# Last chunk's up product over 256 full rows: seven half-width block products in place of eight

## The chip, the core and the metric

The kernel runs on one core of a Trainium2 chip. The metric is the device time of one execution in microseconds (us). Five engines with queues of their own work side by side: TensorE (PE in the profile; its weight loads are listed apart as PEld), VectorE (DVE), ScalarE (ACT), GpSimd (POOL) and SyncE (SP, which here only issues DMAs). Each engine takes its instructions in the order of the program and waits for others through semaphores.

## What is computed

A recurrent attention cell over 4 batches, 8 heads and 768 time steps of 40 dimensions gives `y`; its heads are laid side by side as 3072 tokens of 320 values, and these go through a gated feed-forward block:

```python
x = attn_out.transpose(0, 2, 1, 3).reshape(B * S, H * D)   # 3072 x 320
h = x @ w_in                                               # 320 x 2048
g = h * np.cos(h)
return g @ w_out                                           # 2048 x 320
```

The change concerns `x @ w_in`, called the up product here. `g @ w_out` is the down product.

## The kernel before

The 768 time steps are cut into six chunks of 128. One chunk of all four batches is 512 tokens. While chunk `c` goes through the feed-forward block, the cells of chunk `c + 1` are computed beside it; the last chunk, `c = 5`, has no cell work beside it.

`both_parts(c, b)` runs two of a chunk's eight steps, `f2 = 2b` and `2b + 1`. A step makes 256 of the 2048 columns of `h`, in two PSUM banks of 128 columns by 512 tokens (`pup`, `self.pu[0]` and `[1]`, from a pool of two buffers, so that the next step needs these two banks again). In each step:

- `Up` issues the up product. The 320 rows of `w_in` are two blocks of 128 rows (`w_in_sb`, line 659) and 64 rows that are left over (`w_in_l`, line 653). A block takes the full 512 tokens against 128 columns: four products of 128x512 per step, then two products of 64 rows. Each float32 product is two passes on TensorE, so that the profile counts 8 and 4.
- `near` (ScalarE, line 667) rounds `h`, `rest` (VectorE, line 670) takes the remainder, `sin` (ScalarE, line 675) its sine, and `gate` (VectorE, line 679) multiplies by `h`. This is done for both banks; the last reading of a bank is by `gate`.
- `sums` adds halves of the gated tiles, on VectorE (lines 728 to 731) and beside it on GpSimd (lines 733 to 736). They feed the down product, which is already made of seven block products in place of eight. GpSimd's first sum waits for the second `gate`.
- `down_slot` issues a number of the down product's parts, each of 160 columns (line 769), for earlier steps: the last chunk has 14 for each of its 8 steps. `quota` says how many in which step; the sums of the last step are used after the loop.

At `f2 = 0` of a chunk the 12 products that are left of the chunk before are issued; then `combine_first` and `combine` (lines 781 to 799) add up its four accumulators `X0, X1, Y0, Y1` into the output tiles. They lie in a PSUM pool of four banks. At `f2 = 1` sixteen `late` products of the chunk before follow, in a bank that comes free when `combine` has read `X0` (line 789).

The order of each engine's queue is the order in which the program is written (`tc.manual_schedule()`). In a step of the last chunk it is: up product on TensorE, the four element-wise steps, `sums`, `down_slot`. `x` of a chunk lies in `xT` (blocks of 128 rows, index `NK * b + i`) and `xL` (the 64 rows); line 548 writes the last part of `xT` for the next chunk during step 6 of the chunk before.

Three pools matter here beside these: `raws` (`qr`, `kr`, the raw q and k of two cells at a time), which are last read when the last cells are transposed (line 457); `pe` with tag `E`, three buffers of 128x1024; and GpSimd's queue in chunk 4, which also carries `scale_q` (line 466) and `decay_exponents` (line 391), the latter followed by eight exponentials on ScalarE (line 405).

Of the kernel before, what the change touches and what calls it, by code (L numbers as in the profile page):

```python
# [11 lines left out]
FP = mybir.dt.float32  # L12
# [17 lines left out]
def kernel(  # L30
# [610 lines left out]
    class Up:  # L641


        def __init__(self, c, f2):
            self.c, self.f2 = c, f2
            self.pu = [ps_u.tile([128, B * C], FP, name="pup", tag="up") for _ in range(2)]

            ahead = f2 % 2 == 1 and c < NC - 1

            def low():  # L650
                for e, pu in enumerate(self.pu):
                    r = slice(64 * e, 64 * e + 64)
                    nc.tensor.matmul(pu, w_in_l[r, f2], xL[c][r].rearrange("p b t -> p (b t)"), start=ahead, stop=not ahead)  # L653

            if ahead:
                low()
            for i in range(NK):
                for e, pu in enumerate(self.pu):
                    nc.tensor.matmul(pu.rearrange("p (b t) -> p b t", b=B), w_in_sb[:, i, ts(2 * f2 + e, 128)], xT[c][:, i:NK * B:NK],  # L659
                                     start=(i == 0 and not ahead), stop=(i == NK - 1 and ahead))  # L660
            if not ahead:
                low()
            self.n = [p3.tile([128, B * C], I32, name="n", tag="n") for _ in range(2)]
# [13 lines left out]
        def gate(self, e):  # L677
# [2 lines left out]
                                           op0=OP.mult, op1=OP.mult)  # L680
            gs[self.c, 2 * self.f2 + e] = g

    def down(c, f2):
        if f2 == 0:
            po[c] = [ps_o.tile([128, DM], FP, name="po", tag="o") for _ in range(B)]

        order = [(f, b) for f in (2 * f2, 2 * f2 + 1) for b in range(B)]
        if f2 == NF // 2 - 1:
            order.sort(key=lambda fb: fb[1])
        for f, b in order:  # L690
            nc.tensor.matmul(po[c][b], gs[c, f][:, ts(b, C)], w_out_sb[:, f], start=(f == 0), stop=(f == NF - 1))  # L691
            if f == NF - 1:
                o = out_tile()
                nc.scalar.copy(out=o, in_=po[c][b])
                out_to(c, b, o)
# [11 lines left out]
    def weight_sums(part):  # L707

        if part == 0:
            for i in range(3):  # L710
                T[i] = pc.tile([128, NF // 2, HALF], FP, name=f"T{i}", tag="bits")
        r = ts(part, NF // 8)
        B11, B12, B21, B22 = (wv[:, r, e, h] for e in range(2) for h in range(2))
        T2, T3, T4 = (t[:, r] for t in T)
        nc.gpsimd.tensor_tensor(out=T3, in0=B22, in1=B12, op=OP.subtract)
        nc.gpsimd.tensor_tensor(out=B12, in0=B12, in1=B11, op=OP.subtract)
        nc.gpsimd.tensor_tensor(out=T2, in0=B22, in1=B12, op=OP.subtract)
        nc.gpsimd.tensor_tensor(out=T4, in0=B21, in1=T2, op=OP.subtract)
# [41 lines left out]
    def late_products(c):  # L760
        L = late[c] = ps_o.tile([128, 2, HALF], FP, name="late", tag="o")
        for k in range(NF // 2):
            for i, rhs in ((0, wv[:, k, 0, 1]), (1, wv[:, k, 1, 1])):
                yield L[:, i], Ds[c, k // 4][:, k % 4, i], rhs, k == 0 and i == 0, k == LAST and i == 1

    def run(made, n):
        for _ in range(n):
            a, lhs, rhs, start, stop = next(made)
            nc.tensor.matmul(a, lhs, rhs, start=start, stop=stop)  # L769
# [39 lines left out]

    made_of = {}  # L810

    def down_slot(c, f2):

        if c == 0:
            if f2 > 0:
                down(0, f2 - 1)
            return
        if f2 == 0:
            if c == 1:
                down(0, LAST)  # L820
            else:
                run(made_of[c - 1], 12)
            return
        if f2 == 1 and c > 1:
            run(late_products(c - 1), NF)
            combine_late(c - 1)
            return
        if c not in made_of:
            made_of[c] = all_products(c)
        each = 14 if c == NC - 1 else 12  # L830
        quota = [0] * 8
        for m in range(2, 8):
            quota[m] = each * 7 * (m - 1) // 6 - each * 7 * (m - 2) // 6
        run(made_of[c], each if c == 1 else quota[f2])

    pw, pmu = (ps_u.tile([128, HP, C], FP, name=name, tag="up") for name in ("pw", "pmu"))
# [199 lines left out]
    def both_parts(c, b):  # L1036

        n = (c + 1) * B + b
        cell = n < N
        for i in range(2):  # L1040
            f2 = 2 * b + i
            up = Up(c, f2)
            if cell and i == 0:
                scores(n)
            if cell and i == 1:
                if n % 2 == 1 and n > B + 1 and n + 3 < N:
                    load_two(n + 3, "Kv")
            for e in range(2):
                up.near(e)
            for e in range(2):  # L1050
                up.rest(e)
            if i == 0:
                if cell:
                    weigh(n)
                    if n + 1 < N:
                        decay_exponents(n + 1)
                for e in range(2):
                    up.sin(e)
                    up.gate(e)
                if c > 0:  # L1060
                    sums(c, f2)
                if b == 0 and c == 1:
                    sigmoid(c + 1)

                if c == 0:
                    made = [pieces.pop(0) for _ in range(min(1, len(pieces)))]
                    p, piece = outs.pop(0)
                    made.append(piece)
                    for dst, bits in made:
                        take_apart(dst, bits)  # L1070
                    for dst, bits in made:
                        bound(dst)
                    for dst, bits in made:
                        put_together(dst, bits)
                    load_out(p)
                if cell and n + 1 < N:
                    decay(n + 1)
            else:
                if cell:
                    seam_out(n)  # L1080
                if cell:
                    state(n)
                for e in range(2):
                    up.sin(e)
                    up.gate(e)
                if c > 0:
                    sums(c, f2)
                if n == B + 1:
                    low_dimensions(n + 1)
                if pieces:  # L1090
                    to_float32(*pieces.pop(0))
                if cell and n + 1 < N:
                    if c > 0:
                        weigh_k(n + 1)
                    odd_values(n + 1)
            if i == 1 and b == B - 1 and 0 < c < NC - 2:
                sigmoid(c + 2)
                sin_next()
            down_slot(c, f2)
            if f2 == 0 and c > 1:  # L1100
                for p in range(2):
                    combine_first(c - 1, p)
            if cell and i == 0:
                turn_gate(n)
                values(n)
                seam(n)
                normalize_turned(n)
                fade(n)
                if c == 1 and b < 3:
                    weight_sums(b + 1)  # L1110
                if n % 2 == 1 and n > B + 1 and n + 3 < N:
                    load_two(n + 3, "qk")
                if n > B + 1 and n + 3 < N:
                    load_E(n + 3)
                if b == B - 2 and c + 2 < NC:
                    load_o(c + 2)
                if c == 0 and pieces:
                    to_float32(*pieces.pop(0))
                sin_next()
            if f2 == 0 and c > 1:  # L1120
                for p in range(2):
                    combine(c - 1, p)
            if i == 1:
                if c == 0 and b + 2 < B:
                    pieces.extend(weights_in(b + 2))
                    load_two((n + 3) // 2 * 2)
                    load_E(n + 3)
                if c == 0:
                    turn_blocks(n + 1, "k")
                    p = next_out()  # L1130
                    turn_blocks(n + 1, "q")
                    scale_q(n + 1)
                    weigh_k(n + 1)
                    load_out(p)
                elif cell and n + 1 < N:
                    turn_blocks(n + 1)
                    scale_q(n + 1)
                if (c, f2) == (0, LAST):
                    weight_sums(0)

    pieces, outs = [], []
    with tc.manual_schedule():
# [41 lines left out]
```

## Time and profile before

| | us |
|---|---|
| three runs | 533.92, 536.92, 536.73 (median 536.73) |
| span of the profiled execution (no other time of it is listed) | 535.1 |
| TensorE busy over the span | 519.7 (97%) |
| VectorE, ScalarE, GpSimd busy | 419.1, 287.1, 226.5 |
| chunk 5, from its first up product to the last down product | 453.84 to 529.9 |
| its eight up products, 128-row part | 3.5 each |
| its eight up products, 64-row part | 1.06 each |

A group of the profile is read as: line, engine, operation, tile written and tiles read, shapes, count, busy time and mean of one. In a timeline, the first number is the start in us, the second how long the group took; matmuls overlap their neighbours by their pipeline, so that the distance between two starts is the time that they occupy.

### The profile page before, as it was taken

Reading aid. Unit: us, or ns where it says so; the run is one execution under the profiler, and the core shown is the slowest. Engines: PE = TensorE matmul, PEld = TensorE weight load, DVE = VectorE, ACT = ScalarE, POOL = GpSimd, SP = SyncE. Lnnn points to the kernel's source line nnn. Section 1 sums busy time; section 2 is a strip of 40 time slices with the busy share of each in tenths; the row PEclk is TensorE's granted clock in tenths of the full one; section 3 lists DMA queues with packets and bytes.
Section 4 is the critical chain, followed back from the end, with each engine's and each line's share of the span. In section 5 each row is a group of like instructions: output and inputs, shape, how many; then the busy total and the mean of one; then the engine's idle time right before and its main releaser. Section 6 shows DMA issues by size and latency. Waiting matters only on the chain.

```text
span 535.1 us, 10497 instructions
## 1 busy us (share of the span) xinstructions
PE 519.7 (97%) x3844; PEld 353.6 (66%) x3844; DVE 419.1 (78%) x907; ACT 287.1 (54%) x548; POOL 226.5 (42%) x369
## 2 busy tenths in 40 slices
PE   7999889999999999999999999999999999999996
PEld 4886446556657767667667667667667667576755
DVE  5565988997888888898878898878897878663636
ACT  2586987857556537835537736527835531322221
POOL 7435554654676572632632632632431422121211
PEclk9586989999999999999999999999999999999999
DMA  9998859769949359139159239159210000000001
GB/s 138 233 205 221 256 143 219 172 108 248 174 115 196 40 131 190 45 93 184 40 119 164 54 89 187 38 118 164 56 59 7 2 5 6 26 26 1 0 1 49
DMA packets 99939, 57.81 MB, mean 108 GB/s; under 512 B 62304, under 2 KB 92608, under 8 KB 99888
## 3 DMA queue, kind: packets, MB, share of 16 engines
q1 hardware_dynamic: 96496, 55.64, 48.3%
q10 hardware_dynamic: 3248, 1.33, 1.2%
q8 instruction: 30, 0.49, 0.4%
q14 instruction: 21, 0.17, 0.1%
q0 software_dynamic: 144, 0.18, 0.1%
HBM read 51.71 MB, written 4.11 MB: 104 GB/s over the span
## 4 chain that ended last, share of the span: by engine, by line
PE 85%; DVE 6%; ACT 4%; issue 2%; DMA 2%; POOL 1%; SPq 1%; DVEq 0%; POOLq 0%; ACTq 0%
PE pup L659 28%; PE acc L769 24%; PE pup L653 8%; PE po L691 5%; PE ps L484 4%; PE late L769 3%; PE vt L519 2%; PE ph L500 2%; PE vt L510 2%; PE pu L611 2%; PE pt L434 1%; PE pw L841 1%; DMA bits<-in_moe_w_in_dram 1%; PE pm L376 1%; PE vt L516 1%
## 5 line engine op out<-in xcount | busy, mean ns | idle before, releaser
L659 PE MATMUL pup<-xT,w_in_sb 128*128 128x512 f32 x384 | 176.0, 601 | 0.2
L667 ACT ACTIVATE n<-pup 128x512 int32<-128x512 f32 x96 | 53.8, 593 | 187.1 <-PE pup L653 135.6
L659 PEld LDWEIGHTS pup<-xT,w_in_sb 128*128 128x128 f32 x384 | 70.1, 191 | 86.4 <-issue 84.2
L670 DVE SCALAR_TENSOR_TENSOR n<-pup,n 128x512 f32<-128x512 f32 x96 | 63.1, 687 | 73.0 <-ACT n L667 71.6
L733 POOL TENSOR_TENSOR D<-g 128x128 f32<-128x128 f32 x40 | 19.8, 496 | 217.3 <-DVE g L679 217.3
L675 ACT ACTIVATE n<-n 128x512 f32<-128x512 f32 x96 | 57.6, 627 | 23.1 <-DVE n L670 14.6
L679 DVE SCALAR_TENSOR_TENSOR g<-pup,n 128x512 f32<-128x512 f32 x96 | 61.7, 684 | 3.9 <-ACT n L675 3.3
L769 PE MATMUL acc<-w_out_sb,g 128*128 128x160 f32 x320 | 58.6, 304 | 0.0
L769 PE MATMUL acc<-T,g 128*128 128x160 f32 x320 | 58.0, 301 | 0.1
L653 PE MATMUL pup<-xL,w_in_l 64*128 64x512 f32 x192 | 54.2, 641 | 0.0
L769 PEld LDWEIGHTS acc<-w_out_sb,g 128*128 128x128 f32 x320 | 47.7, 190 | 5.6 <-issue 4.2
L769 PEld LDWEIGHTS acc<-T,g 128*128 128x128 f32 x320 | 48.1, 190 | 3.7 <-issue 3.0
L405 ACT ACTIVATE E<-E,tab 128x128 f32<-128x128 f32 x160 | 49.0, 388 | 0.3
L691 PE MATMUL po<-w_out_sb,g 128*128 128x320 f32 x128 | 37.7, 449 | 4.1 <-POOL w_out_sb L165 4.1
L691 PEld LDWEIGHTS po<-w_out_sb,g 128*128 128x128 f32 x128 | 24.7, 196 | 16.3 <-POOL w_out_sb L165 5.1
L769 PE MATMUL acc<-T,S 128*128 128x160 f32 x160 | 35.0, 300 | 0.0
L484 PEld LDWEIGHTS ps<-t,t 40*128 40x128 f32 x384 | 25.8, 195 | 12.7 <-DVE t L457 6.5
L490 DVE TENSOR_TENSOR E<-ps,E 128x512 f32<-128x512 f32 x48 | 30.7, 681 | 0.6 <-PE ps L484 0.5
L965 ACT ACT_TABLE_LOAD x23 | 29.5, 1283 | 2.2 <-DVE w_out_sb L158 1.8
L653 PEld LDWEIGHTS pup<-xL,w_in_l 64*128 64x128 f32 x192 | 14.4, 184 | 23.0 <-issue 20.5
L484 PE MATMUL ps<-t,t 40*128 40x128 f32 x384 | 27.6, 285 | 1.6 <-DVE t L457 1.6
L769 PE MATMUL acc<-w_out_sb,S 128*128 128x160 f32 x160 | 28.7, 299 | 0.0
(175 smaller groups left out, 881.4 us busy)
## 6 DMA issues: line engine op xcount, KB each, us to landing
E<-M_d SPq DMA_DIRECT2D x22, 512.0 KB
qr<-in_q_dram SPq DMA_DIRECT2D x36, 160.0 KB
kr<-in_k_dram SPq DMA_DIRECT2D x36, 160.0 KB
G<-G_d SPq DMA_DIRECT2D x20, 256.0 KB
bits<-in_moe_w_out_dram SPq DMA_DIRECT2D x8, 640.0 KB
bits<-in_moe_w_in_dram SPq DMA_DIRECT2D x32, 128.0 KB
out_dram<-o_sb SPq DMA_DIRECT2D x24, 160.0 KB
ks<-in_k_dram SPq DMA_DIRECT2D x10, 320.0 KB
```

The costliest lines, as they stand in the source:

```text
L405: nc.scalar.activation(out=Es[n][:, h], in_=Es[n][:, h], func=AF.Exp, scale=-1.0, bias=tab[:, c, 0, g:g + 1])
L484: nc.tensor.matmul(ps[j][:, p], kT[r, p], qT[r, p], start=True, stop=True)
L490: nc.vector.tensor_tensor(out=w, in0=pss[n][j], in1=w, op=OP.mult)
L653: nc.tensor.matmul(pu, w_in_l[r, f2], xL[c][r].rearrange("p b t -> p (b t)"), start=ahead, stop=not ahead)
L659: nc.tensor.matmul(pu.rearrange("p (b t) -> p b t", b=B), w_in_sb[:, i, ts(2 * f2 + e, 128)], xT[c][:, i:NK * B:NK], start=(i == 0 and not ...
L667: nc.scalar.activation(out=self.n[e], in_=self.pu[e], func=AF.Copy, bias=0.25)
L670: nc.vector.scalar_tensor_tensor(out=self.n[e].bitcast(FP), in0=self.pu[e], scalar=0.25, in1=self.n[e], op0=OP.add, op1=OP.subtract)
L675: nc.scalar.activation(out=r, in_=r, func=AF.Sin, scale=TWO_PI_DOWN)
L679: nc.vector.scalar_tensor_tensor(out=g, in0=self.pu[e], scalar=TWO_PI, in1=self.n[e].bitcast(FP), op0=OP.mult, op1=OP.mult)
L691: nc.tensor.matmul(po[c][b], gs[c, f][:, ts(b, C)], w_out_sb[:, f], start=(f == 0), stop=(f == NF - 1))
L769: nc.tensor.matmul(a, lhs, rhs, start=start, stop=stop)
L965: nc.scalar.activation(out=spot, in_=spot, func=AF.Sin)
```

## The change

In chunk 5 alone `UpFast` takes the place of `Up`. The 256 full rows by 256 columns by 512 tokens of a step are seen as two by two blocks, `A` (rows by columns) and `X` (rows by the tokens of two batches each). Seven products of 128 rows, 128 columns and 256 tokens are made of sums of blocks, in place of eight; the 64 rows that are left over are added as before. The parts:

- `up_weight_sums` makes four sums of `w_in`'s blocks on GpSimd, for all eight steps at once (128x1024 each), in the buffers of raw q and k: two behind step 1 of chunk 4, two behind step 5.
- `x_sums` makes four sums of chunk 5's blocks of `x` on GpSimd (128x256 each), behind step 7 of chunk 4; the last one is written over a block of `xT`. The first product of chunk 5 reads the second sum, its second product the fourth.
- In each step four products are made (two per bank), both banks are copied to SBUF by ScalarE (`s`, 128x1024), two down products (`fill_in`) are issued between in steps 1 to 7, and the other three products and the 64 rows are added on in the banks.
- Two adds on GpSimd and one on VectorE, 256 wide each, join the copies; VectorE adds one of them to half of bank 0 (in place) and one to bank 1 (into `s`). `near`, `rest` and `gate` read the second half of `h` from `s`.
- The quotas of down products in chunk 5 move by a few toward the end, and two of each step are issued by `fill_in`.

```diff
+    wi = w_in_sb.rearrange("p i (f e n) -> p i f e n", e=2, n=128)
+    A11, A12, A21, A22 = (wi[:, i, :, e] for e in range(2) for i in range(NK))
+    HB = B // 2 * C
+    fast = NC - 1
...
+    def up_weight_sums(part):
+        tt = nc.gpsimd.tensor_tensor
+        if part == 0:
+            S1, S2, S4, S3 = Sw.setdefault(0, [raws[w][m][:, 0:NF // 2 * 128].rearrange("p (f n) -> p f n", n=128)
+                                               for m in range(2) for w in "qk"])
+            tt(out=S1, in0=A21, in1=A22, op=OP.add)
+            tt(out=S2, in0=S1, in1=A11, op=OP.subtract)
+        else:
+            S1, S2, S4, S3 = Sw[0]
+            tt(out=S3, in0=A11, in1=A21, op=OP.subtract)
+            tt(out=S4, in0=A12, in1=S2, op=OP.subtract)
...
+    def x_sums(c):
+        T1, T2, T4 = Tx[c] = pe.tile([128, H, C], FP, name="Tx", tag="E")[:, 0:3 * B // 2].rearrange("p (k b) t -> k p b t", k=3)
+        tt = nc.gpsimd.tensor_tensor
+        tt(out=T1, in0=x_block(c, 0, 1), in1=x_block(c, 0, 0), op=OP.subtract)
+        tt(out=T2, in0=x_block(c, 1, 1), in1=T1, op=OP.subtract)
+        tt(out=T4, in0=x_block(c, 1, 0), in1=T2, op=OP.subtract)
+        tt(out=x_block(c, 0, 1), in0=x_block(c, 1, 1), in1=x_block(c, 0, 1), op=OP.subtract)
+
+    class UpFast(Up):
+        def __init__(self, c, f2, fill):
...
+            product(b1, second, S2, T2, True, True)
+            product(b1, first, S3, X[0][1], stop=True)
+            product(b0, first, A11, X[0][0], True, True)
+            product(b0, second, S1, T1, stop=True)
+            s = pe.tile([128, H, C], FP, name="Sx", tag="E").rearrange("p (k b) t -> p k (b t)", k=4)
+            nc.scalar.copy(out=s[:, 2:4], in_=b1.rearrange("p (k n) -> p k n", k=2))
+            nc.scalar.copy(out=s[:, 0:2], in_=b0.rearrange("p (k n) -> p k n", k=2))
+            fill()
+            product(b1, first, A22, T4)
+            product(b0, first, A12, X[1][0])
+            product(b0, second, S4, X[1][1])
+            for e, pu in enumerate(self.pu):
+                r = slice(64 * e, 64 * e + 64)
+                nc.tensor.matmul(pu, w_in_l[r, f2], xL[c][r].rearrange("p b t -> p (b t)"), start=False, stop=True, skip_group_check=True)
+            nc.gpsimd.tensor_tensor(out=s[:, 1], in0=s[:, 1], in1=s[:, 0], op=OP.add)
+            nc.vector.tensor_tensor(out=s[:, 0], in0=s[:, 0], in1=s[:, 3], op=OP.add)
+            nc.gpsimd.tensor_tensor(out=s[:, 3], in0=s[:, 1], in1=s[:, 2], op=OP.add)
+            nc.vector.tensor_tensor(out=b0[:, second], in0=b0[:, second], in1=s[:, 0], op=OP.add)
+            h = s[:, 0:4:3]
+            nc.vector.tensor_tensor(out=h, in0=b1.rearrange("p (k n) -> p k n", k=2), in1=h, op=OP.add)
...
+    FILL = 2
+    lates = {}
+
+    def fill_in(c, f2):
+        if f2 == 1:
+            lates[c] = late_products(c - 1)
+            run(lates[c], FILL)
+        elif f2 > 1:
+            if c not in made_of:
+                made_of[c] = all_products(c)
+            run(made_of[c], FILL)
...
-            run(late_products(c - 1), NF)
+            if c >= fast:
+                run(lates[c], NF - FILL)
+            else:
+                run(late_products(c - 1), NF)
...
+        if c == NC - 1:
+            quota = [0, 0, 14, 15, 15, 15, 15, 24]
+        if c >= fast:
+            quota = [max(0, m - FILL) for m in quota]
...
-            up = Up(c, f2)
+            up = UpFast(c, f2, lambda: fill_in(c, f2)) if c >= fast else Up(c, f2)
...
+                if c == fast - 1 and b in (0, 2):
+                    up_weight_sums(b // 2)
+                if c == fast - 1 and b == B - 1:
+                    x_sums(c + 1)
```

More of the change, by code (lines that the diff above doesn't have):

```diff
@@ L681, in gate @@
             gs[self.c, 2 * self.f2 + e] = g
+    wi = w_in_sb.rearrange("p i (f e n) -> p i f e n", e=2, n=128)
+    A11, A12, A21, A22 = (wi[:, i, :, e] for e in range(2) for i in range(NK))
+    HB = B // 2 * C
+    fast = NC - 1
+    Sw, Tx = {}, {}
+    def up_weight_sums(part):
[9 more added lines that the diff above has]
+            tt(out=S4, in0=A12, in1=S2, op=OP.subtract)
@@ new lines, in x_block @@
+    def x_block(c, i, t):
+        h = NK * B // 2
+        return xT[c][:, i + h * t:h * (t + 1):NK]
+    def x_sums(c):
[5 more added lines that the diff above has]
+        tt(out=x_block(c, 0, 1), in0=x_block(c, 1, 1), in1=x_block(c, 0, 1), op=OP.subtract)
@@ new lines, with product, near, rest @@
+    class UpFast(Up):
+        def __init__(self, c, f2, fill):
+            self.c, self.f2 = c, f2
+            self.pu = [ps_u.tile([128, B * C], FP, name="pup", tag="up") for _ in range(2)]
+            (S1, S2, S4, S3), (T1, T2, T4) = Sw[0], Tx[c]
+            b0, b1 = self.pu
+            first, second = slice(0, HB), slice(HB, 2 * HB)
+            def product(bank, part, w, x, start=False, stop=False):
+                nc.tensor.matmul(bank[:, part].rearrange("p (b t) -> p b t", b=B // 2), w[:, f2], x, start=start, stop=stop, skip_group_check=True)
+            X = [[x_block(c, i, t) for t in range(2)] for i in range(NK)]
+            product(b1, second, S2, T2, True, True)
[18 more added lines that the diff above has]
+            nc.vector.tensor_tensor(out=h, in0=b1.rearrange("p (k n) -> p k n", k=2), in1=h, op=OP.add)
+            self.n = [p3.tile([128, B * C], I32, name="n", tag="n") for _ in range(2)]
+            self.h = h
+        def near(self, e):
+            if e == 0:
+                return super().near(e)
+            nc.scalar.activation(out=self.n[e].rearrange("p (k n) -> p k n", k=2), in_=self.h, func=AF.Copy, bias=0.25)
+        def rest(self, e):
+            if e == 0:
+                return super().rest(e)
+            n = self.n[e].rearrange("p (k n) -> p k n", k=2)
+            nc.vector.scalar_tensor_tensor(out=n.bitcast(FP), in0=self.h, scalar=0.25, in1=n, op0=OP.add, op1=OP.subtract)
+        def gate(self, e):
+            if e == 0:
+                return super().gate(e)
+            g = gp.tile([128, B * C], FP, name="g", tag="g")
+            nc.vector.scalar_tensor_tensor(out=g.rearrange("p (k n) -> p k n", k=2), in0=self.h, scalar=TWO_PI,
+                                           in1=self.n[e].rearrange("p (k n) -> p k n", k=2).bitcast(FP), op0=OP.mult, op1=OP.mult)
+            gs[self.c, 2 * self.f2 + e] = g
```

## The prediction

> **What bounds the kernel now.** I read the busy shares first (TensorE 97%), then the chain of waits, which runs over TensorE's products from chunk 4 to the end, then the timelines of chunk 5, engine by engine. TensorE's:
>
> ```profile
> 453.84 3.60 PE L659 MATMUL pup<-xT,w_in_sb 128*128 128x512 f32 x8
> 457.36 1.13 PE L653 MATMUL pup<-xL,w_in_l 64*128 64x512 f32 x4
> 458.42 0.81 PE L769 MATMUL acc<-w_out_sb,g 128*128 128x160 f32 x4
> ...
> 461.79 3.60 PE L659 MATMUL pup<-xT,w_in_sb 128*128 128x512 f32 x8
> 465.31 1.13 PE L653 MATMUL pup<-xL,w_in_l 64*128 64x512 f32 x4
> 466.37 4.61 PE L769 MATMUL late<-w_out_sb,D 128*128 128x160 f32 x32
> 470.82 3.60 PE L659 MATMUL pup<-xT,w_in_sb 128*128 128x512 f32 x8
> ```
>
> The starts follow each other without a gap: here every TensorE microsecond saved is one off the end, and every wait put into this queue is one on it. GpSimd and VectorE around the seam of chunks 4 and 5:
>
> ```profile
> 453.56 0.46 POOL L733 TENSOR_TENSOR D<-g 128x128 f32<-128x128 f32 x1 [8.14 <-DVE g L679]
> 454.10 0.46 POOL L734 TENSOR_TENSOR S<-D,g 128x128 f32<-128x128 f32 x1
> 454.63 0.45 POOL L735 TENSOR_TENSOR D<-g,S 128x128 f32<-128x128 f32 x1
> 455.04 0.50 POOL L736 TENSOR_TENSOR g<-g 128x128 f32<-128x128 f32 x1
> ```
>
> ```profile
> 448.90 0.56 DVE L548 TENSOR_TENSOR xT<-yt,db 128x384 f32<-128x384 f32 x1
> ...
> 463.64 0.54 DVE L731 TENSOR_TENSOR g<-g 128x128 f32<-128x128 f32 x1
> 464.10 0.48 DVE L789 TENSOR_TENSOR o_sb<-acc,o_sb 128x320 f32<-128x320 f32 x1
> ```
>
> GpSimd's four sums of chunk 4's last step end at 455.54, 1.7 us after TensorE has begun chunk 5. The last is a gap of TensorE early in the run, with the clock after it (columns: PE busy, PEld, DVE, ACT, POOL, then the granted clock):
>
> ```profile
> 74.00:75.00 1.00, 0.00 (x0) 0.00 (x0) 0.46 (x1) 1.00 (x1) 0.41 (x1) 1.00 0.15 42
> 75.00:76.00 1.00, 0.00 (x0) 0.00 (x0) 0.10 (x1) 0.99 (x4) 1.00 (x1) 0.81 0.05 15
> 76.00:77.00 1.00, 0.80 (x2) 0.61 (x3) 1.00 (x2) 0.72 (x2) 1.00 (x2) 0.50 0.33 112
> ...
> 78.00:79.00 1.00, 1.00 (x3) 0.64 (x2) 1.00 (x3) 1.00 (x3) 1.00 (x2) 0.50 1.05 296
> 79.00:80.00 1.00, 1.00 (x5) 0.73 (x4) 0.97 (x3) 1.00 (x2) 0.42 (x1) 0.98 1.11 229
> ```
>
> **The products.** Eight passes of 512 columns take 457.36 - 453.84 = 3.52 us, 0.44 each or 0.86 ns a column; in the down products four passes of 160 columns stand 0.544 us apart, 0.136 each or 0.85 ns a column. So time goes with columns even where weights change every 0.136 us, and a pass of 256 is 0.219, a product (two passes) 0.437. Seven are 3.06: **0.46 saved in each step, 3.7 in eight**. The 64 rows stay at 1.06. The number of down products is unchanged.
>
> **The sums of x.** They are queued on GpSimd behind lines 733 to 736, which wait for the second gate of chunk 4's last step; that `xT` is whole at 449.46 doesn't help them. No row is 256 wide. Sums of 128 take 0.46 here, those of 320 (lines 715 to 718) 0.87 to 0.97, those of 512 (line 466) 1.27; between 128 and its neighbours that gives 0.74, and I take it, with the 0.07 that lies between dependent sums. The second sum ends at 455.60 + 2 x 0.74 + 0.07 = 457.15, the fourth at 458.75. The first product therefore starts at 457.2 in place of 453.84 (3.36 lost), takes 0.44, and the second waits from 457.64 to 458.8 (1.16): **4.5 lost**. Nothing else is in TensorE's queue there. With 0.46 a sum it is 3.4, with 0.97 it is 5.4.
>
> **Copies.** Rows like them are `near`'s, 512 wide out of PSUM: 0.60, beginning 0.16 after the product's end. From the fourth product's end to the second copy's end is 0.76 + 0.05. In steps 1 to 7 two down products (0.54) and the fifth product (0.44) cover it: nothing. Step 0 has no fill: **0.4 lost** (0 to 0.6).
>
> **The adds.** GpSimd: 0.74, then VectorE 0.42 (line 568, 256 wide: 0.425), then GpSimd 0.74: ready 2.0 after the second copy, some 4.6 after the step's start; the up product ends at 4.66, so TensorE hides them. VectorE's add into half of bank 0 lies on the path (lines 798 and 789: 0.32 for 160, 0.48 for 320 columns out of PSUM; 0.42 for 256, with its wait 0.45). The add of bank 1 (0.68, like line 670) runs beside `near` of bank 0. So everything behind the up product comes 0.45 later. In steady steps the first gate ended 2.9 after the up product's end and now ends 3.4; bank 0 is needed again after 13 products and two of the next step, 3.54 + 0.87 = 4.4. Hidden, with 1.0 to spare; if the adds took 0.97 on GpSimd, still hidden.
>
> **Fill at step 1.** The two `late` products, formerly behind the whole up product, now stand behind four of its seven, and their bank is `X0`, read last by line 789. Before, that ended 464.58 - 458.42 = 6.2 after step 0's up product; it stays behind step 0's element-wise work and sums on VectorE, so now 6.65. TensorE arrives after 12 x 0.272 + 4 x 0.437 = 5.0: **1.7 lost** (1.2 to 2.0 with the add's bounds). Who queues behind it: the rest of step 1's up product, and its chain. The `late` bank in turn was read out 6.5 after step 1's up product (line 806); with 0.45, and 0.85 that step 1's adds lose behind `combine` on VectorE, that is 7.8, and step 2 wants it after 14 products, its up product and four more: 3.8 + 4.66 + 1.1 = 9.6. Free.
>
> **The weight sums** in chunk 4. At 1024 wide the slope from 128 to 512 (2.1 ns a column) gives 2.35 each, the steepest row (0.97 at 320) 3.1. The first two run from 400.0, behind line 466, to 404.9 and push line 391's select from 399.97 to 404.95, then ScalarE's eight exponentials from 402.96 to 406.1 and the table load behind them to 409.8. `near` of the next step was called at 410.35: hidden, by 0.3, and the banks were free another 0.75 before TensorE wanted them. At 3.1 each it costs 0.45. Step 2's sums on GpSimd end 2.7 later; their products follow 411. The other two lie in a gap (438.5 to 443.4; the next GpSimd work began at 443.43): **0**.
>
> **The end.** TensorE waited 0.27 before the last 11 products (526.40 to 526.67) for line 731's last sum, 5.76 after the up product. Now 6.2 after it, but 25 products at 0.272 = 6.8 lie between: **0.3 gained**.
>
> **The clock.** In the windows above TensorE lay idle from 73.57 to 76.20; the clock fell to half at 75.62 and came back at 79.04, 3.4 later. Going back by such stretches, the one before the fall was idle for 60%. The stretch of 61.97 to 65.39 was idle for 41% and the clock stayed. The seam will have 0.44 of work in 5.0 us: wherever the stretches lie, one of them is idle for about 60% or more. Then up to 3.4 us run at half speed, 1.7 lost when the fall meets the first busy moment, 0.9 when it came 1.6 earlier, less what the copies' wait hides: **1.0** (0 to 1.7).
>
> The Trainium skill, TensorE: Matmul & The Clock Gate, Part 1, says that the array falls to half speed after at least one idle window of about 3.4 us; by that rule the seam's single product breaks the idle time and the clock stays, which is the first rival below. The trace does not agree with so strict a reading: the clock fell within a gap of 2.6 us.
>
> **Sum:** -3.7 + 4.5 + 0.4 + 1.7 - 0.3 + 1.0 = +3.6 on a span of 535.1. The page lists no other time of that execution; its span lies between the three runs, 1.6 below their median. On the median: 536.7 + 3.6 = 540.3.
>
> **Rivals.**
> 1. The clock stays at full speed: +2.6, 539.3. For it: 41% idle did nothing. Against: the fall after 60%.
> 2. Faster: the seam holds no wait, as if the sums of `x` were done by 453.84, and the fill finds its bank: -4.0, 532.7; with the bank's wait and step 0's copy still there -1.9, 534.8. For it: `xT` is whole 4.4 us earlier and GpSimd is 81% idle in the stage. Against: the queue's order.
> 3. Slower by over 1%: the clock falls a second time. The wait at `X0` is 1.7 of a 3.4 us stretch, 50%, between the 41% that did nothing and the 60% that did; past that point another 1.7 are lost, and with the first fall at its dearest it is +6.0, 542.7. Sums of `x` at 0.97 would add 0.9 to any case.
> 4. The change doesn't save what it says: passes of 256 no shorter than 0.25 each, so that seven products cost what eight did: 544.0. Against: 160 columns at 0.136.
>
> **Numbers.** Forecast 52%, rival 1 22%, rival 2 9%, rival 3 14%, rival 4 3%. 1% is 5.4 us, about what a measurement of this kernel can tell from no change: under 531.4 is faster, over 542.1 slower. Rival 2 reaches 532.7, which only the runs' own spread (3.0) takes past the bound: 3%. Rivals 3 and 4 and the forecast's upper end: 18%. The range reaches from 536.0 (rival 1 with sums at 0.46 and a low median) to 543.2.
>
> **What would show it.** In the timeline of TensorE: the first L725 product near 457.2 and the second near 458.8; a wait of about 1.7 ahead of the first `late` product; seven products plus the 64 rows in 4.12 us and no waits in steps 2 to 7; no wait near the end; the clock at 0.5 for about 3.4 us near 458 to 462. Wrong would be: sums of `x` ahead of lines 733 to 736's counterparts, waits in each steady step (then the adds on GpSimd or the copies are late), or `near` of chunk 4's step 3 late behind the exponentials.

## The result and the profile after

| | before | after |
|---|---|---|
| median of 12 runs | 536.83 | 538.49 |
| lowest to highest | 533.92 to 537.55 | 536.72 to 541.73 |
| span of the profiled execution | 535.1 | 536.8 (its own time 538.55) |
| TensorE busy | 519.7 (97%) | 513.7 (96%) |
| VectorE, ScalarE, GpSimd busy | 419.1, 287.1, 226.5 | 432.2, 297.0, 250.4 |

The ratio of after to before is 1.006, with a 95% interval of 1.004 to 1.008: 3.2 us slower (2.1 to 4.3). That is not the quotient of the two medians, 1.003: the runs of each kernel fall into a shorter and a longer group (means 534.4 and 537.0 before, 537.7 and 541.1 after), and the median before lies in the longer group, the median after in the shorter. The 6 us between the two busy times of TensorE don't measure the change either: in two further profiles of the kernel before (below) TensorE was busy for 514.7 and for 521.5.

The single runs of one kernel lie 3 to 5 us apart, and in the profiles that scatter lies ahead of chunk 5: the seam, the end of chunk 4's last down product, came at 453.84 before the change and at 451.65 after it, though the diff adds nothing to TensorE's queue before it; the same kernel profiled again has its seam up to 4 us elsewhere (below). I therefore compare one stretch of TensorE from here on: from the seam to the end of the last down product. Its last group before the change:

```profile
529.22 0.71 PE L769 MATMUL late<-w_out_sb,D 128*128 128x160 f32 x4
```

A group of four passes ends 0.54 after its start, so before the change the stretch runs from 453.84 to 529.22 + 0.54, **75.92 us**. TensorE's timeline after the change, around the seam and at the last group:

```profile
451.10 0.71 PE L856 MATMUL acc<-T,g 128*128 128x160 f32 x4
454.93 0.70 PE L725 MATMUL pup<-Tx,kr 128*128 128x256 f32 x2 [3.12 <-POOL Tx L710]
456.41 1.22 PE L725 MATMUL pup<-xT,kr 128*128 128x256 f32 x2 [0.78 <-POOL xT L712]
457.43 1.06 PE L725 MATMUL pup<-xT,w_in_sb 128*128 128x256 f32 x2
458.28 1.06 PE L725 MATMUL pup<-Tx,qr 128*128 128x256 f32 x2
459.13 0.86 PE L725 MATMUL pup<-Tx,w_in_sb 128*128 128x256 f32 x2
460.01 0.70 PE L725 MATMUL pup<-xT,w_in_sb 128*128 128x256 f32 x2
...
466.79 0.59 PE L725 MATMUL pup<-Tx,qr 128*128 128x256 f32 x2
468.31 0.81 PE L856 MATMUL late<-w_out_sb,D 128*128 128x160 f32 x4 [0.93 <-DVE o_sb L876]
468.96 0.59 PE L725 MATMUL pup<-Tx,w_in_sb 128*128 128x256 f32 x2
...
530.87 0.71 PE L856 MATMUL late<-w_out_sb,D 128*128 128x160 f32 x4
```

It runs from 451.65 to 531.41, **79.76 us: 3.84 more**. Where the queue stood without a gap there are now three: ahead of the first product, waiting for GpSimd's second sum of `x` (line 710); ahead of the second, waiting for the fourth (line 712); and ahead of the two `late` products, waiting for VectorE's last reading of `X0` (line 876, before 789). From the second product to the sixth the starts stand 0.85 apart and more, those of later steps 0.43. In the table of stretches of the same kernel (PE busy, PEld, DVE, ACT, POOL, granted clock) the reason shows:

```profile
452.82:456.23 3.41, 0.70 (x2) 0.30 (x2) 0.68 (x2) 0.00 (x0) 3.25 (x6) 1.00 0.00 0
456.23:459.65 3.42, 3.24 (x8) 2.53 (x8) 0.00 (x0) 0.86 (x2) 0.13 (x1) 0.50 0.00 0
459.65:463.00 3.35, 3.33 (x16) 1.85 (x15) 1.06 (x3) 0.55 (x2) 1.45 (x2) 1.00 0.02 5
```

The clock is at half for one stretch of 3.42 us, right behind one in which TensorE had a single product to do. GpSimd's timeline after the change, to be held against its lines of before:

```profile
451.37 0.45 POOL L820 TENSOR_TENSOR D<-g 128x128 f32<-128x128 f32 x1 [8.14 <-DVE g L679]
451.90 0.45 POOL L821 TENSOR_TENSOR S<-D,g 128x128 f32<-128x128 f32 x1
452.44 0.45 POOL L822 TENSOR_TENSOR D<-g,S 128x128 f32<-128x128 f32 x1
452.85 0.50 POOL L823 TENSOR_TENSOR g<-g 128x128 f32<-128x128 f32 x1
453.31 0.76 POOL L709 TENSOR_TENSOR Tx<-xT 128x256 f32<-128x256 f32 x1
454.15 0.72 POOL L710 TENSOR_TENSOR Tx<-xT,Tx 128x256 f32<-128x256 f32 x1
454.95 0.72 POOL L711 TENSOR_TENSOR Tx<-xT,Tx 128x256 f32<-128x256 f32 x1
455.63 0.72 POOL L712 TENSOR_TENSOR xT<-xT 128x256 f32<-128x256 f32 x1
```

The sums of chunk 4's last step (820 to 823) wait for its second gate and hold the sums of `x` behind them, though these had their input 4 us earlier, at 446.72 + 0.56:

```profile
446.72 0.56 DVE L548 TENSOR_TENSOR xT<-yt,db 128x384 f32<-128x384 f32 x1
```

### The profile page after: what moved, and what is told of

Its sections match the earlier page's. It is cut to its first block, busy times and chain, and to the rows that moved or that the text cites. A ratio compares the mean times of both kernels' runs of the same rounds, so it can differ in the third digit from the quotient of the medians.

```text
span 536.8 us, 10651 instructions
## 1 busy us (share of the span) xinstructions
PE 513.7 (96%) x3892; PEld 358.6 (67%) x3892; DVE 432.2 (81%) x931; ACT 297.0 (55%) x564; POOL 250.4 (47%) x393
## 4 chain that ended last, share of the span: by engine, by line
PE 83%; DVE 5%; ACT 4%; DMA 3%; issue 2%; POOL 1%; ACTq 0%; SPq 0%; DVEq 0%; POOLq 0%
PE acc L856 24%; PE pup L659 22%; PE pup L653 7%; PE po L778 5%; PE pup L725 4%; PE ps L484 4%; PE late L856 3%; PE vt L519 2%; PE vt L510 2%; PE pup L741 2%; PE pu L611 1%; PE pw L948 1%; PE ph L500 1%; DMA bits<-in_moe_w_out_dram 1%; DMA bits<-in_moe_w_in_dram 1%
## 5 line engine op out<-in xcount | busy, mean ns | idle before, releaser
L659 PE MATMUL pup<-xT,w_in_sb 128*128 128x512 f32 x320 | 146.4, 600 | 0.4 <-ACT xT L622 0.2
L667 ACT ACTIVATE n<-pup 128x512 int32<-128x512 f32 x88 | 49.9, 593 | 157.1 <-PE pup L653 85.4
L659 PEld LDWEIGHTS pup<-xT,w_in_sb 128*128 128x128 f32 x320 | 58.0, 189 | 74.6 <-issue 72.4
L670 DVE SCALAR_TENSOR_TENSOR n<-pup,n 128x512 f32<-128x512 f32 x88 | 58.2, 687 | 44.8 <-ACT n L667 43.4
L679 DVE SCALAR_TENSOR_TENSOR g<-pup,n 128x512 f32<-128x512 f32 x88 | 56.8, 684 | 2.5 <-ACT n L675 1.9
L778 PE MATMUL po<-w_out_sb,g 128*128 128x320 f32 x128 | 39.6, 466 | 6.4 <-POOL w_out_sb L165 6.4
L653 PE MATMUL pup<-xL,w_in_l 64*128 64x512 f32 x160 | 45.2, 641 | 0.0
L778 PEld LDWEIGHTS po<-w_out_sb,g 128*128 128x128 f32 x128 | 25.8, 206 | 19.4 <-POOL w_out_sb L165 7.4
L856 PEld LDWEIGHTS acc<-T,S 128*128 128x128 f32 x160 | 26.2, 190 | 3.0 <-issue 3.0
```

The lines of the kernel that those rows point to most:

```text
L667: nc.scalar.activation(out=self.n[e], in_=self.pu[e], func=AF.Copy, bias=0.25)
L670: nc.vector.scalar_tensor_tensor(out=self.n[e].bitcast(FP), in0=self.pu[e], scalar=0.25, in1=self.n[e], op0=OP.add, op1=OP.subtract)
L679: nc.vector.scalar_tensor_tensor(out=g, in0=self.pu[e], scalar=TWO_PI, in1=self.n[e].bitcast(FP), op0=OP.mult, op1=OP.mult)
```

## The experiments

The theory: the products do what they should, and two waits that the change puts into TensorE's queue, with the clock that falls over the first of them, cost more than the products save. The rivals: the clock falls because of the products themselves, the `late` products wait for something else, and waits that are taken away come back elsewhere. All numbers on TensorE are stretches from the seam to the last down product; the seam is read as above in each profile.

**Sums of `x` early.** They are issued as soon as `xT` is whole, in step 6 of chunk 4, ahead of the sums of step 7.

```diff
                 normalize_turned(n)
+                if c == fast - 1 and b == B - 1:
+                    x_sums(c + 1)
                 fade(n)
...
-                if c == fast - 1 and b == B - 1:
-                    x_sums(c + 1)
```

> The four sums of x are issued on GpSimd right after the last part of x is written, ahead of the sums of chunk 4's last step; nothing else changes. Measure: the stretch of TensorE from the end of chunk 4's last down product (the seam) to the end of the last down product, 75.9 us before the change and 79.8 after it. Theory (the queue's order makes the two waits of 3.28 and 1.05, and they make the clock fall, 1.5): no wait ahead of the first two products, clock 1.0 throughout, stretch 79.8 - 5.8 = 74.0; the device time 2 us under the kernel before. Rival A (the seam's wait is not the sums but the weights' sums, the banks or the copies): the first product still begins 2 us or more after the seam, stretch over 77. Rival B (the clock falls for another reason, such as the narrow products themselves): no waits, but clock 0.5 for 3.4 us in chunk 5, stretch 75.5.

Measured: 533.96 us (530.28 to 536.46), 0.9974 of the kernel before (0.9945 to 1.0002), which by itself is not clear of no change. The stretch is 450.99 to 524.95, **73.96**. TensorE's timeline:

```profile
450.99 0.59 PE L725 MATMUL pup<-Tx,kr 128*128 128x256 f32 x2
451.42 0.59 PE L725 MATMUL pup<-xT,kr 128*128 128x256 f32 x2
451.86 0.59 PE L725 MATMUL pup<-xT,w_in_sb 128*128 128x256 f32 x2
452.29 0.59 PE L725 MATMUL pup<-Tx,qr 128*128 128x256 f32 x2
452.72 0.67 PE L725 MATMUL pup<-Tx,w_in_sb 128*128 128x256 f32 x2
453.56 0.70 PE L725 MATMUL pup<-xT,w_in_sb 128*128 128x256 f32 x2 [0.16 <-ACT Sx L734]
```

No wait ahead of the first two products, 0.43 from each to the next, and the clock at 1.0 throughout chunk 5. So the queue's order was the cause, and the narrow products don't lower the clock: both rivals fall. The sixth product comes 0.84 after the fifth in place of 0.43: that is the 0.41 for ScalarE's second copy. In the changed kernel it can hardly be seen, because those products stand 0.85 apart anyway at the half clock (459.13 to 460.01 is 0.88, and the copy ended at 459.96).

**Seam kept busy.** The waits stay; TensorE is given products of zeros meanwhile.

```diff
+            if f2 == 0:
+                idle = ps_a.tile([128, HP, C], FP, name="idle", tag="a")
+                warm(14, idle)
             product(b1, second, S2, T2, True, True)
+            if f2 == 0:
+                warm(4, idle)
             product(b1, first, S3, X[0][1], stop=True)
```

> As the changed kernel, with 14 products of zeros (128x512, bf16, 0.22 us each) into a spare bank ahead of chunk 5's first product and 4 between the first and the second; both waits stay. Theory (the idle TensorE makes the clock fall): the first two products start where they did, 3.3 and 4.8 us after the seam, the granted clock stays 1.0, and the 1.5 us of half speed are gone: stretch from the seam to the last down product 79.8 - 1.5 = 78.3. Rival (the clock falls because of what products run, not because of the gap): clock 0.5 for 3.4 us as before, stretch 79.8 or a little more.

Measured: 537.63 us (536.55 to 541.02), 1.0044 of the kernel before (1.0016 to 1.0071). The stretch is 453.72 to 532.13, **78.41**. TensorE's first two products, then the table of stretches over the first 10 us behind the seam:

```profile
457.02 0.70 PE L725 MATMUL pup<-Tx,kr 128*128 128x256 f32 x2
458.50 0.70 PE L725 MATMUL pup<-xT,kr 128*128 128x256 f32 x2
```

```profile
453.70:457.00 3.30, 3.21 (x16) 1.27 (x13) 1.81 (x4) 0.00 (x0) 3.03 (x6) 1.00 0.00 0
457.00:460.50 3.50, 3.48 (x14) 2.05 (x14) 0.00 (x0) 0.98 (x2) 1.40 (x2) 1.00 0.00 0
460.50:464.00 3.50, 3.34 (x17) 2.12 (x17) 1.33 (x3) 0.70 (x2) 1.44 (x2) 1.00 0.02 5
```

The two products start 3.30 and 4.78 after the seam, as in the changed kernel (3.28 and 4.76), but the clock stays at 1.0. So the half-speed stretch came of the gap, and its price is 79.76 - 78.41 = 1.35 by itself.

**Bank read first.** VectorE's last reading of `X0` is issued ahead of step 0's sums; the 12 products and ScalarE's copies, which it needs, move with it in the text, and TensorE's order stays.

```diff
...
+                if c >= fast and b == 0:
+                    down_slot(c, f2)
+                    for p in range(2):
+                        combine_first(c - 1, p)
+                    combine(c - 1, 0, True)      # its first addition alone
                 if c > 0:
                     sums(c, f2)
...
-            down_slot(c, f2)
-            if f2 == 0 and c > 1:
+            if not (c >= fast and f2 == 0):
+                down_slot(c, f2)
+            if f2 == 0 and 1 < c < fast:
...
```

> As the changed kernel, with VectorE's first addition of the combination (the last reading of X0) issued ahead of the sums of chunk 5's step 0 in place of behind them. Theory (the two late products in step 1's up product wait for this bank): the wait of 1.09 ahead of them is gone, stretch from the seam to the last down product 79.8 - 1.1 = 78.7. Rival (they wait for ScalarE's copies or for the sums of step 0): the wait stays, or moves behind them to the fifth product, stretch 79.8.

Measured: 537.57 us (535.42 to 541.87), 1.0049 of the kernel before (1.0020 to 1.0078); against the changed kernel's 1.006 that alone decides nothing. The stretch does: 451.70 to 530.42, **78.72**. TensorE's timeline at the place:

```profile
466.84 0.59 PE L725 MATMUL pup<-Tx,qr 128*128 128x256 f32 x2
467.27 0.71 PE L856 MATMUL late<-w_out_sb,D 128*128 128x160 f32 x4
467.81 0.59 PE L725 MATMUL pup<-Tx,w_in_sb 128*128 128x256 f32 x2
```

The `late` products follow the fourth product without a gap, and no gap comes behind them in this step (one of 0.06 comes in step 2): the wait was for the bank alone, and 1.04 of the 1.09 are won.

**Both at once.**

> Both edits at once: sums of x early, X0 read ahead of the sums of step 0. Theory (the waits are independent): stretch from the seam to the last down product 79.8 - 5.8 - 1.1 = 72.9, 3.0 below the kernel before (75.9), with only the copies' wait of 0.4 in step 0 left; device time 3 us under the kernel before. Rival (the queue gives it back: without the seam's wait, step 0's chain or the bank recycling becomes late): waits of 0.5 us or more in other steps, stretch 74 or more.

Measured: **532.55 us** (530.38 to 535.98), 0.9945 of the kernel before (0.9915 to 0.9975): 3.0 us faster than the kernel before (1.3 to 4.6), and none of the others tried is clearly faster. TensorE's first and last group of the stretch:

```profile
451.44 0.59 PE L725 MATMUL pup<-Tx,kr 128*128 128x256 f32 x2
...
523.84 0.71 PE L856 MATMUL late<-w_out_sb,D 128*128 128x160 f32 x4
```

It is 451.44 to 524.38, **72.94**, so that the two savings add up: 5.80 and 1.04 alone, 6.82 together. Nearly nothing is given back elsewhere (a wait of 0.06 in step 2).

**No fill.** On that kernel, `FILL = 0`: the two down products are no longer put between the fourth and fifth product of a step.

> On the kernel with both edits (sums of x early, X0 read first; stretch 72.94): no down products between the fourth and the fifth product of a step; they stay in the step's own slot. Theory (the two fill products and the fifth product hide the second copy): steps 1 to 7 each get the wait that step 0 has now, 0.41 ahead of the sixth product, seven in all: stretch 72.9 + 2.9 = 75.8. Rival (the copies are late or early for another reason, so that the fill hides nothing): stretch 72.9 to 73.3, no wait ahead of the sixth product.

Measured in one run: 534.31 us; the stretch is 450.73 to 527.08, **76.35**. Step 1, TensorE:

```profile
460.51 0.67 PE L725 MATMUL pup<-Tx,w_in_sb 128*128 128x256 f32 x2
461.35 0.70 PE L725 MATMUL pup<-xT,w_in_sb 128*128 128x256 f32 x2 [0.16 <-ACT Sx L734]
```

Each of steps 1 to 7 gets the wait of step 0: 0.84 between these two starts in place of 0.43. The seven together cost 3.4, somewhat more than 7 x 0.41 = 2.9: a step without fill takes 4.68 (467.92 to 472.60), and one with it 4.71 (475.32 to 480.03 in the changed kernel) with 0.545 of down products inside, so 4.17 without them; the difference is 0.51. The remaining 0.1 a step is the longer spacing of the products next to the gap. The fill hides the copy, as forecast.

**All covered.** Step 0 gets a fill as well (two of the 12 products), and `X0` is read between its two gates, since TensorE arrives earlier.

```diff
...
-        if f2 == 1:
+        if f2 == 0:
+            run(made_of[c - 1], FILL)
+        elif f2 == 1:
...
-                run(made_of[c - 1], 12)
+                run(made_of[c - 1], 12 - FILL if c >= fast else 12)
...
                     up.sin(e)
+                    if c >= fast and b == 0 and e == 1:
+                        down_slot(c, f2)
+                        combine_first(c - 1, 0)
+                        combine(c - 1, 0, True)
                     up.gate(e)
+                if c >= fast and b == 0:
+                    combine_first(c - 1, 1)
...
```

> On the same kernel: step 0 gets its fill too, two of the twelve products left of chunk 4, and X0 is read still earlier, between the two gates of step 0, since TensorE now arrives 0.54 sooner. Theory: the 0.41 wait of step 0 is gone and no other comes, stretch 72.9 - 0.4 = 72.5, device time 3.3 us under the kernel before. Rival (the second gate, now half a microsecond later, or X0, is waited for): a wait of 0.2 or more ahead of the first late product or in step 1, stretch 72.8 or more.

Measured: 533.72 us (530.68 to 537.03), 0.9951 of the kernel before (0.9921 to 0.9982). The stretch is 451.50 to 524.37, **72.87**, not 72.5: the rival was right. TensorE in step 2:

```profile
468.10 0.59 PE L725 MATMUL pup<-xT,kr 128*128 128x256 f32 x2
469.02 0.70 PE L725 MATMUL pup<-xT,w_in_sb 128*128 128x256 f32 x2 [0.33 <-DVE g L679]
```

Step 0's wait is gone, and 0.49 are lost here (469.02 in place of 468.53). VectorE's timeline of this kernel says why step 1's first gate is late:

```profile
464.73 0.33 DVE L892 TENSOR_TENSOR o_sb<-acc,o_sb 128x160 f32<-128x160 f32 x1
464.97 0.42 DVE L743 TENSOR_TENSOR Sx<-Sx 128x256 f32<-128x256 f32 x1
465.49 0.43 DVE L745 TENSOR_TENSOR pup<-pup,Sx 128x256 f32<-128x256 f32 x1
466.23 0.69 DVE L747 TENSOR_TENSOR Sx<-pup,Sx 128x512 f32<-128x512 f32 x1 [0.30 <-POOL Sx L744]
```

Step 1's adds (743 to 747) stand in VectorE's queue behind the combination of chunk 4, which ends with line 892 at the same moment as in the kernel with both edits (464.75 there). When TensorE came 0.4 earlier, VectorE did not, and the wait moved. That the combination is what holds it was not tried by moving it.

**The same kernels once more.** Two further profiled runs of the kernel before and one of the changed kernel, each with no edit, say whether the stretch is a property of the kernel and the seam's place is not.

> The kernel before, profiled once more as a control. Theory (the time ahead of the seam scatters from run to run; the stretch behind it does not): the seam anywhere from 450 to 454, the stretch from the seam to the last down product 75.9 to within 0.1. Rival (the change also moves what lies ahead of the seam by 2 us): the seam again at 453.8 to within 0.5.

> The same once more, on the same chip: the seam at another place by up to 3 us, the stretch again 75.9 to within 0.1; by the rival the seam at 453.8 again.

> The changed kernel once more. Theory: the seam anywhere from 450 to 454, the waits of 3.28, 1.05 and 1.09 behind it as before to within 0.1; the clock's part (1.35) depends on where its stretches lie against the seam and may be 0.9 to 1.7, so that the stretch is 79.3 to 80.2. Rival: the seam at 451.6 again to within 0.5.

Measured, one run each: the kernel before in 534.53 and 538.51 us, the changed one in 539.07. TensorE's timeline in the first further run of the kernel before, its seam (the start of chunk 5's first product, with no wait ahead of it) and its last group:

```profile
451.47 3.60 PE L659 MATMUL pup<-xT,w_in_sb 128*128 128x512 f32 x8
...
526.85 0.71 PE L769 MATMUL late<-w_out_sb,D 128*128 128x160 f32 x4
```

The seam is at 451.47 and the stretch 75.92; in the second run they are 455.44 and 75.93. The two times differ by 3.98 and the two seams by 3.97: the scatter between runs lies ahead of chunk 5. The changed kernel's second profile has its seam at 452.18, the first product 3.28 after it, the second 1.05 late, 1.08 ahead of the `late` products, and a stretch of 79.75, which puts the clock's price at 79.75 - 78.41 = 1.34. The rival's seam of 453.8 before did not come; that of 451.6 after was missed by little (452.18). Between kernels the stretch therefore counts to about 0.01 in these profiles, and the +3.84 is the change's.

The scatter is older than anything that the change adds. From the seventh time that GpSimd runs `scale_q` (line 466) to the seam it is 274.44 to 274.48 us in all eleven profiles, of every kernel here (179.38 to 453.84 before, 177.20 to 451.65 after), and the first weight sum stands inside that time. The two further runs of the kernel before are 3.99 apart by the third `scale_q` already (97.01 and 101.00), and the granted clock over their first 100 us is 0.93 and 0.85. What sets the clock there was not tried. Of the timed difference 3.2 - 3.84 = -0.6 (-1.7 to +0.5) lies outside the stretch, and that interval holds zero.

## Why the prediction was right, and which of its terms were off

| term | forecast | measured |
|---|---|---|
| products, eight steps | -3.7 | -3.4 |
| two waits at the seam | +4.5 | +4.33 |
| copy in step 0 | +0.4 | +0.41 (with the sums early) |
| wait for `X0` | +1.7 | +1.09 |
| clock | +1.0 | +1.35 |
| end | -0.3 | -0.27 |
| weight sums, adds | 0 | 0 |
| sum | +3.6 | +3.5; the stretch itself +3.84 |

The forecast of 540.3 lies 1.8 above the median of 538.49, inside its range; the step from before to after, +3.6, was measured as +3.84 in the stretch, as +3.2 by the ratio and as +1.7 by the medians. The steps were as forecast: the waits, what ends each of them and the clock's fall. That the sum came within 0.3 of the stretch is partly luck, for the terms were off by up to 0.6 and their errors nearly cancel. The copy's 0.41 and the clock's 1.35 don't count the same time twice: with the seam kept busy, from which the 1.35 is taken, the copy's wait stands open (459.90 to 460.74).

About 0.3 of the stretch is in no term. It is the products right behind a gap: with the seam kept busy they stand 0.54 apart in place of 0.43 at two places (458.50 and 460.74) and 0.65 in place of 0.54 at a third (469.04), 0.1 each. The forecast had counted the gaps alone.

- Products: 4.17 for a step in place of 4.59, 0.42 saved and not 0.46. The 64 rows begin 0.52 after the seventh product (478.45 to 478.97), where the other products stand 0.43 apart; that spacing the forecast had not counted. Rival 4 is wrong with it: a pass of 256 takes 0.215 and not 0.25.
- Seam: 451.65 to 454.93 is 3.28, and the second product began 1.05 later than it could have (456.41 against 454.93 + 0.43). The price of a sum of 256, taken between its neighbours at 0.74, is 0.72 to 0.76. The experiment that moves the sums removes these waits whole.
- `X0`: the term was too large by 0.6 because of the sums on VectorE ahead of it. They were taken as they ran before, 2.12 (462.06 to 464.18); after, they took 1.50 (466.36 to 467.86). The 0.45 for VectorE's add was right: `near` began 0.63 after the up product (462.13 to 462.76) where it had been 0.16.
- Clock: the mean of 1.0 lay below the 1.35 that came, inside its bounds of 0 to 1.7. In the three profiles that have the fall it comes 4.5 to 4.8 behind the seam, so that they don't show what another place of the stretches would cost. The rule of the Trainium skill (TensorE: Matmul & The Clock Gate, Part 1), that the array falls to half after at least one idle window of about 3.4 us, does not hold in the strict reading: the stretch before the fall had a product of 0.43 in it and the one early in the run was busy for 40%. That makes the first rival wrong. The second fall of rival 3 did not come: behind 459.65 the clock stayed at 1.0, over the wait at `X0` as well.
- Adds and copies: no step from 2 on has a wait in the changed kernel, so GpSimd's two adds and the copies are hidden, and the run without fill shows what hides the copies.
- The weight sums took 2.37 and 2.36 (forecast 2.35). `near` of chunk 4's step 3 was released by TensorE, 0.47 after ScalarE was free, and from the start of GpSimd's line 466 in chunk 4's step 1 to the seam it is 55.09 us in both profiles (398.75 to 453.84 and 396.56 to 451.65). Hidden, as forecast.
- The rival on the fast side, that the seam holds no wait, is what the edits make true: its second figure, -1.9 with the bank's wait and the copy left, was met by the early sums (73.96 - 75.92 = -1.96), and its best, -4.0, was approached by both edits (-2.98: the copy's 0.41 is left, the products saved 0.3 less, and the rest is the small wait in step 2 and the spacing behind the two gaps).

## What to carry to other kernels

Where one engine's queue is full, price a change by its queue and not by its work: here 3.4 us of products were saved, and two waits at the seam (4.33), one at a bank (1.09) and the clock that fell over the first two (1.35) took twice that. The waits were for inputs that could have been ready, but were made, or were read for the last time, behind other work in another engine's order. The last producer before the first use sets the price; when a sum's input is ready early, issue it there, ahead of the work that waits for something later. The gap at the seam, 4.8 us with one product in it, cost 1.35 more than itself through the clock; look at the granted clock behind such a gap. And when a wait is taken away, ask which queue did not get earlier with it.

## What was not expected of the hardware

VectorE's additions of two tiles in SBUF became up to four times as long while GpSimd ran. In chunk 4's step 2, VectorE's timeline after the change, then GpSimd's:

```profile
399.90 1.28 DVE L679 SCALAR_TENSOR_TENSOR g<-pup,n 128x512 f32<-128x512 f32 x2
401.57 1.17 DVE L815 TENSOR_TENSOR S<-g 128x128 f32<-128x128 f32 x1 [0.39 <-PE acc L856]
402.77 1.06 DVE L816 TENSOR_TENSOR S<-S,g 128x128 f32<-128x128 f32 x1
403.87 0.43 DVE L817 TENSOR_TENSOR S<-g,S 128x128 f32<-128x128 f32 x1
```

```profile
400.24 2.36 POOL L696 TENSOR_TENSOR kr<-qr,w_in_sb 128x1024 f32<-128x1024 f32 x1
402.55 1.14 POOL L391 TENSOR_SCALAR_AFFINE_SELECT E<-E 128x1024 f32<-128x1024 f32 x1
```

The first addition took 0.30 at the same place before the change, the second 0.51. The first runs beside the weight sum and ends 0.14 after it (402.74 and 402.60), the second beside the select and ends 0.14 after that (403.83 and 403.69); in three further profiles with the change (sums of `x` early, both at once, the changed kernel again) the distance is 0.14 or 0.15 each time. So the rows look less like a slower addition than like one that waits for GpSimd's instruction to end. The gates, which read one operand from PSUM, took 1.28 for two in both kernels, and GpSimd's sum was not longer than the one before it (2.36 and 2.37), which ran beside no addition of two tiles in SBUF. The Trainium skill (GPSIMD Engine Reference, Specifications) says that GpSimd's SBUF interfaces are shared with VectorE and that it contends with VectorE instructions that have two SBUF inputs; the rows agree, and show that here it is VectorE that waits. Among the small sums of a step the engine that starts first goes unhindered: in step 0 after the change VectorE began 0.05 ahead of GpSimd (466.36 and 466.41), and its first sum took 0.29, GpSimd's 0.56; in step 2 GpSimd began 0.03 ahead (484.30 and 484.33), and its sum took 0.45, VectorE's 0.57. All this is read from rows and was not tried by itself; by these rows it is what made the wait for `X0` shorter than forecast.
